# A written-out instruction order, numbered buffers and a finer softmax chain in a fused attention and highway kernel

## The chip, the cores and the metric

The kernel runs on one core of one Trainium2 chip. The core has five engines with instruction streams of their own: TensorE (PE in the profile, with its weight loads as PEld), VectorE (DVE), ScalarE (ACT), GpSimd (POOL) and SyncE (SP). Sixteen DMA engines move data between HBM and the core's memories; here GpSimd issues all loads and SyncE all stores. The metric is the device time in microseconds. The profile of one execution shows a span, from the first to the last instruction, which is a little shorter than the time.

## The reference

Four batches of N = 6336 rows with C = 256 channels. Channel attention: q and k are normalized over the rows, their 256 x 256 product is put through a softmax, and v is multiplied by it. The result x, 25344 rows of 256, goes through a highway layer.

```python
qn = q / (np.linalg.norm(q, axis=1, keepdims=True) + 1e-06)
kn = k / (np.linalg.norm(k, axis=1, keepdims=True) + 1e-06)
s = kn.transpose(0, 2, 1) @ qn / tau                 # [B, 256, 256]
a = np.exp(s - s.max(-1, keepdims=True))
a /= a.sum(-1, keepdims=True) + 1e-09
x = (v @ a).reshape(B * N, C)
H = np.maximum(x @ w_h, 0.0)
T = 1.0 / (1.0 + np.exp(-(x @ w_t + b_t)))
out = T * H + (1.0 - T) * x                          # float32
```

All inputs and the output are float32 in HBM, 25.95 MB for each of q, k, v and the output.

## The kernel before

Each batch has two stages. Stage 1 runs over 50 steps of 128 (at the end 96) rows and accumulates k'q, and the diagonals of k'k and q'q, in two PSUM banks. In batches 1 to 3, for the first five of the six chunks of eight steps, the sum of q squares is not made on TensorE: ScalarE squares and GpSimd adds. Then a chain of small operations makes the norms, the softmax and three 256 x 256 weight matrices in one tile pair `mr`: for x itself (times -0.5), for x w_h and for x w_t. Stage 2 runs over 25 tasks of 256 rows per batch, 100 tasks g in all: v is transposed, and three products h, t and d (x) are made, four matmuls of 256 columns each; ScalarE computes a halved relu into d's bank and a tanh, VectorE combines. Loads cast float32 to float16 on the way.

Everything is a task with engine, estimated duration, dependencies and buffers. A simulation at build time (`Plan.run`) picks, for each engine, the ready task with the lowest priority number, and the instructions are emitted in that order. At run time every engine runs its own instructions in order.

```python
QK_BUFS = 5; V_BUFS = 5; O_BUFS = 7; LAG = 5; UNTIL = 73; APART = 5
BY_DMA = 3          # last batch: chunks 3 to 6 of v are transposed by DMA
PRIO = {"tr": (24.974, 16.445, 34.195, 63.304), ...}      # offsets by kind and batch

def new(tag, shape, dt, name):
    return pool_of.get(tag, work).tile(shape, dt, tag=tag, bufs=nbuf[tag], name=name)

# [cut] first loads: q, k of batch 0, then
for s in range(0, CH, CH // 2):
    plan_load("q", 1, 0, s, CH // 2)
    plan_load("k", 1, 0, s, CH // 2)
w_ld = [...]                       # the two weight matrices
plan_load("v", 0, 0)

def stage1(b, s):                  # one step
    for c in range(2):
        nc.tensor.matmul(sg[c][:, 0:C], kc, qa, start=first, stop=False)
        nc.tensor.matmul(sg[c][:, C : C + P], kc, kc, start=False, stop=False)
        if not apart(b, s // CH):
            nc.tensor.matmul(sg[c][:, C + P : C + 2 * P], qa[:, cs], qa[:, cs], start=False, stop=last)

def sum_squares(b, j, step):       # GpSimd, per chunk of eight steps
    if step == 0:   add(out=sq, in0=sq, in1=other)                              # 1024 columns
    elif step == 1: add(out=sq[:, 0:2, :], in0=sq[:, 0:2, :], in1=sq[:, 2:4, :])  # 512
    else:                                                                       # 256, twice
        add(out=sq[:, 0, :], in0=sq[:, 0, :], in1=sq[:, 1, :])
        add(out=sums[b], in0=sums[b], in1=sq[:, 0, :])

# the chain of a batch
dq = dve(lambda: (diagonal(0), diagonal(1), rest_of_q()), ...)
nq = pool(lambda: norm(0), ...)                 # power 0.5 on GpSimd
dk = dve(lambda: (diagonal(2), diagonal(3)), ...)
nk = pool(lambda: norm(2), ...)
plan.loads_stop.append((stop, nk))              # no load is issued until nk is done
gs = act(copy_g, ...)                           # both halves, after dk
iq = dve(lambda: (recip(0), dcat()), ...)       # dcat: 2 x identity times inverse norm
ik = dve(lambda: recip(2), ...)
def recip(n):
    inv = st["inv"][:, n : n + 2]
    nc.vector.tensor_scalar(out=inv, in0=inv, scalar1=1e-6, scalar2=None, op0=AluOp.add, ...)
    nc.vector.reciprocal(out=inv, in_=inv)
def bcast():
    nc.tensor.matmul(st["cqb"], ones, st["dcat"][:, :, :], start=True, stop=True)
# [cut] scale, exp, transpose, recip_sum
def soft(c):                                    # x weights, VectorE
    nc.vector.tensor_scalar(out=mr_t[b][c][:, 0:C], in0=st["e"][:, c, :],
        scalar1=st["ri"][:, c : c + 1], scalar2=-0.5, op0=AluOp.mult, op1=AluOp.mult)
def evac_ah(c, e):                              # h and t weights, 512 columns at once
    o, a, r = mr_t[b][c][:, C : 3 * C], st["ah", c], st["ri"][:, c : c + 1]
    if e == "ACT": nc.scalar.mul(out=o, in_=a, mul=r)
    else:          nc.vector.tensor_scalar(out=o, in0=a, scalar1=r, ...)

# stores: chunk n is held back until chunk n + LAG has been begun (while that is at most UNTIL)
def hold(b, j):
    nc.sync.dma_start(out=held_row, in_=og[(b, j)][0:1, 0, :])

for x in plan.run():
    if x.fn is not None:
        x.fn()
```

Of the kernel before, what the change touches and what calls it, by code (L numbers as in the profile page):

```python
# [15 lines left out]
P = 128  # L16
# [6 lines left out]
AHEAD = 16  # L23
BY_DMA = 3
SHORT = 1.08
MOVE = 165e3
APART = 5
V_AHEAD = 2


PRIO = {
    "tr": (24.974, 16.445, 34.195, 63.304),
    "ev": (74.59, 73.008, 67.512, 50.704),
    "h": (-53.39, -86.015, -64.208, -14.641),
    "bias": (-28.394, 23.065, -1.772, 4.453),
    "t": (4.111, -1.918, 67.766, 74.312),
    "relu": (46.555, -20.175, -1.498, 14.915),
    "x": (0.958, -19.433, 43.343, -6.4),
    "gate": (-54.132, 37.28, -94.231, -112.222),
    "prod": (-40.861, -10.819, -26.763, -55.482),  # L40
    "res": (53.604, 18.42, 116.457, -9.113),
    "s1": (117.419, 42.459, 84.45),
    "sq": (-15.195, 72.384, 19.395),
}
POW = 0.75
HEAD = 5.5
TAIL = 66
EV = BIAS = ("ACT", "DVE")
ENDS = [18, 48.5, 62.25]


class Ring:


    def __init__(self, bufs):
        self.bufs = bufs
        self.freed = []

    def open_at(self, t):
        n = len(self.freed) - self.bufs  # L60
        return n < 0 or (self.freed[n] is not None and self.freed[n] <= t)


class Task:
# [3 lines left out]

    def __init__(self, eng, key, pitch, lat, deps, fn, take=(), drop=(), size=0, follows=()):
        self.eng, self.key, self.pitch, self.lat = eng, key, pitch, lat
        self.deps, self.fn, self.take, self.drop, self.size = deps, fn, take, drop, size
        self.follows = follows
        self.start = self.done = None
        self.late = 0.0
        self.soft = 0
        self.held = {}
        self.serial = False

    def engines(self):
        return self.eng if isinstance(self.eng, tuple) else (self.eng,)

    def settle(self, e):
        n = self.eng.index(e)
        self.pitch, self.lat = self.pitch[n], self.lat[n]
        self.fn = partial(self.fn, e)
        self.eng = e


class Plan:

# [8 lines left out]
    def __init__(self):  # L101
        self.tasks = []
        self.rings = {}

        self.loads_stop, self.sums_stop = [], []

    def ring(self, tag, bufs):
        self.rings[tag] = Ring(bufs)

    def add(self, *args, **kw):  # L110
        t = Task(*args, **kw)
        self.tasks.append(t)
        return t

    def run(self):
        queues = {"POOL": [], "SP": []}
        in_order = {"POOL": [], "SP": []}
        users, followers = {}, {}
        for n, x in enumerate(self.tasks):
            x.n, x.left, x.at = n, len(x.deps) + len(x.follows), 0.0  # L120
            for d in x.deps:
                users.setdefault(d, []).append(x)
            for d in x.follows:
                followers.setdefault(d, []).append(x)
            if x.size or x.serial:
                in_order[x.eng].append(x)
        for lst in in_order.values():
            lst.sort(key=lambda x: (x.key, x.n), reverse=True)
        engines = list(dict.fromkeys(x.eng for x in self.tasks if not isinstance(x.eng, tuple)))
        avail = {e: [x for x in self.tasks if e in x.engines() and not x.left and not (x.size or x.serial)] for e in engines}  # L130
        free = dict.fromkeys(engines, 2.1)
        lanes, order, events = [], [], [0.0, 2.1]
        t, left = 0.0, len(self.tasks)
        eps = 1e-6

        def ready(x):
            return (
                not x.left
                and x.at <= t + eps
                and all(self.rings[g].open_at(t + eps) for g in x.take)  # L140
                and (x.eng != "POOL" or not x.size or sum(d > t + eps for d in lanes) < self.LANES)
            )

        def finish(x, when):
            x.done = when
            events.append(when)
            for owner, tag in x.drop:
                self.rings[tag].freed[owner.held[tag]] = when
            release(users.get(x, ()), when)

        def release(us, when):
            for u in us:
                u.left -= 1
                u.at = max(u.at, when)
                if not u.left and not (u.size or u.serial):
                    for e in u.engines():
                        avail[e].append(u)

        def pick(e):
            quiet = held(self.sums_stop)  # L160
            best = min(
                (x for x in avail[e] if ready(x) and not (quiet and x.soft >= quiet)),
                key=lambda x: (x.key, x.n), default=None,
            )
            lst = in_order.get(e)
            if best is None and lst and ready(lst[-1]) and not (e == "POOL" and held(self.loads_stop)):
                return lst[-1]
            return best

        def held(stops):  # L170
            return next(
                (
                    n + 1 for n, (a, b) in enumerate(stops)
                    if a.start is not None and (b.done is None or b.done > t + eps)
                ),
                0,
            )

        while left or any(queues.values()):
            for e in engines:  # L180
                x = pick(e) if free[e] <= t + eps else None
                if x is None:
                    continue
                if x.size or x.serial:
                    in_order[e].pop()
                else:
                    for other in x.engines():
                        avail[other].remove(x)
                    if isinstance(x.eng, tuple):
                        x.settle(e)  # L190
                left -= 1
                x.start = t
                order.append(x)
                for g in x.take:
                    x.held[g] = len(self.rings[g].freed)
                    self.rings[g].freed.append(None)
                free[e] = t + x.pitch
                release(followers.get(x, ()), free[e])
                events.append(max(free[e], t + 2 * eps))
                if x.size:  # L200
                    queues[e].append([x, float(x.size), t + self.HEAD])
                    events.append(t + self.HEAD)
                    if e == "POOL":
                        x.lane = len(lanes)
                        lanes.append(1e9)
                else:
                    finish(x, t + x.lat)

            act = [qq for qq in queues.values() if qq and qq[0][2] <= t + eps]
            share = self.RATE / max(1, len(act))  # L210
            nxt = [x for x in events if x > t + eps] + [t + qq[0][1] / share for qq in act]
            assert nxt, "no task can start"
            nxt = min(nxt)
            for qq in act:
                qq[0][1] -= share * (nxt - t)
            t = nxt
            events = [x for x in events if x > t - eps]
            for qq in act:
                if qq[0][1] < 1.0:
                    x = qq.pop(0)[0]  # L220
                    finish(x, t + self.LAG + x.late)
                    if x.eng == "POOL":
                        lanes[x.lane] = t + self.LAG
        self.end = max(x.done for x in order)
        return order
# [3 lines left out]
def kernel(  # L229
# [37 lines left out]
        "sq": 2, "vT": 3, "vT_t": 1, "o": O_BUFS, "ot": 1, "uu": 3, "pp": 3, "vtsb": 9, "mr0": 2, "mr1": 2,  # L267
        "sg0": 1, "sg1": 1, "vt": 1, "t": 1, "h": 2, "d": 2,
# [6 lines left out]

    def new(tag, shape, dt, name):
        return pool_of.get(tag, work).tile(shape, dt, tag=tag, bufs=nbuf[tag], name=name)
# [64 lines left out]
    def plan_load(nm, b, j, s=0, n=CH):  # L342

        size = P * n * C * 4 if j < NJ else TR * 2 * C * 4
        tag = nm if j < NJ else f"tail_{nm}"
        x = plan.add(
            "POOL", len(plan.tasks), 0.54, 0, [], lambda: load(nm, b, j, s, n),
            take=[tag] if s == 0 else [], size=size * (1 if j < NJ and n > 2 else SHORT),
        )
        ld.setdefault((nm, b, j), []).append(x)  # L350
# [71 lines left out]
    def natural(b):  # L422

        return b == B - 1
# [670 lines left out]
```

## Time and profile before

Median 270.56 us of three runs (270.31 to 271.51); the span of the profile is 268.3 us.

| Part | Value |
|---|---|
| PE busy | 246.4 us (92%), 2430 matmuls |
| PEld busy | 216.6 us (81%) |
| VectorE busy | 181.6 us (68%) |
| ScalarE busy | 195.1 us (73%) |
| GpSimd busy | 131.7 us (49%) |
| granted TensorE clock, mean | 0.997 |
| first store issued | 101.0 us |
| last load issued | 221.3 us |
| last store issued | 264.6 us |

The page gives the busy share of each engine over 40 equal slices, one digit each in tenths; the DMA queues with the share of sixteen engines' time that their packets took; and a chain of waits, followed back from the last instruction. The windows cut the span into stretches. A busy TensorE there includes the overlap of pipelined matmuls, so a full row does not mean peak rate; the count of instructions beside it tells more.

### The profile page before, as it was taken

What the parts mean: (1) busy time and instruction counts of PE and PEld (TensorE: products, weight loads), DVE (VectorE), ACT (ScalarE), POOL (GpSimd) and SP (SyncE); (2) the same over time, 40 slices, a digit from 0 to 9 for tenths busy, and PEclk for the clock granted to TensorE, in tenths of its full rate; (3) what the DMA queues carried; (4) which work ended last, traced back from release to release, by engine and by line L of the source; (5) the groups of instructions that cost most, each with busy time, mean ns of one, the idle gap of its engine ahead of it and who ended that gap; (6) DMA issues with size and microseconds to landing.
All of it is one profiled execution on the core that took longest, in us unless ns stands there. A gap on an engine that the chain in (4) does not pass through costs nothing.

```text
span 268.3 us, 6249 instructions
## 1 busy us (share of the span) xinstructions
PE 246.4 (92%) x2430; PEld 216.6 (81%) x2430; DVE 181.6 (68%) x377; ACT 195.1 (73%) x365; POOL 131.7 (49%) x167
## 2 busy tenths in 40 slices
PE   0697977999999999999999999999999999999991
PEld 0596864889989978999999878999998778888880
DVE  1000035777766789557878797586878998998994
ACT  1001016978888789999898887787798999998980
POOL 7233468688778064695689138567655110000000
PEclk9999999999999999999999999999999999999998
DMA  6999999999999999999999999999999999999995
GB/s 107 215 211 208 206 206 202 212 213 214 214 213 212 213 214 255 247 263 269 275 286 258 267 267 254 249 236 281 287 280 239 284 214 304 379 399 165 351 423 232
DMA packets 24622, 67.24 MB, mean 251 GB/s; under 512 B 9104, under 2 KB 11280, under 8 KB 21648
## 3 DMA queue, kind: packets, MB, share of 16 engines
q0 software_dynamic: 13472, 39.20, 75.0%
q1 hardware_dynamic: 11120, 27.64, 29.0%
q8 instruction: 19, 0.31, 0.4%
q14 instruction: 11, 0.09, 0.1%
HBM read 78.38 MB, written 25.95 MB: 389 GB/s over the span
## 4 chain that ended last, share of the span: by engine, by line
PE 76%; DMA 12%; ACT 5%; POOL 2%; issue 2%; DVE 2%; ACTq 0%; DVEq 0%; POOLq 0%
PE h L800 16%; PE t L800 16%; PE d L800 15%; PE sg L452 12%; DMA k<-in_k_dram 10%; PE sg L453 6%; PE vtps L760 5%; DMA v<-in_v_dram 2%; ACT uu L854 2%; PE sg L455 2%; PE t L831 1%; PE vtps L754 1%; PE ah L689 1%; POOL q L327 1%; ACT d L840 1%
## 5 line engine op out<-in xcount | busy, mean ns | idle before, releaser
L800 PEld LDWEIGHTS <-vtsb 128*128 128x128 f16 (+1 forms) x1044 | 98.8, 99 | 17.3 <-issue 3.2
L452 PE MATMUL sg<-q,k 128*128 128x256 f16 x384 | 83.8, 277 | 12.7 <-DMA k<-in_k_dram 12.6
L861 DVE SCALAR_TENSOR_TENSOR pp<-uu,d 128x512 f32<-128x512 f32 (+1 forms) x100 | 68.0, 684 | 28.4 <-PE d L800 16.1
L453 PE MATMUL sg<-k 128*128 128x128 f16 x384 | 76.8, 223 | 0.0
L854 ACT ACTIVATE uu<-t 128x512 f32<-128x512 f32 (+1 forms) x100 | 59.7, 597 | 19.1 <-PE t L800 18.5
L880 DVE SCALAR_TENSOR_TENSOR o<-h,pp 128x512 f32<-128x512 f32 x96 | 65.5, 686 | 1.7
L840 ACT ACTIVATE d<-h 128x512 f32<-128x512 f32 (+1 forms) x100 | 57.9, 584 | 5.7 <-PE h L800 4.9
L800 PE MATMUL t<-mr,vtsb 128*128 128x256 f16 (+1 forms) x348 | 52.2, 272 | 1.5 <-ACT t L533 1.2
L800 PE MATMUL h<-mr,vtsb 128*128 128x256 f16 (+1 forms) x348 | 51.2, 272 | 0.5 <-ACT vtsb L533 0.5
L800 PE MATMUL d<-mr,vtsb 128*128 128x256 f16 (+1 forms) x348 | 51.5, 272 | 0.1
L452 PEld LDWEIGHTS <-k 128*128 128x128 f16 x384 | 38.0, 99 | 16.7 <-DMA k<-in_k_dram 13.9
L476 POOL TENSOR_TENSOR sq<-sq,sq 128x1024 f32<-128x1024 f32 x15 | 35.4, 2361 | 16.7 <-ACT sq L470 16.6
L453 PEld LDWEIGHTS <-k 128*128 128x128 f16 x384 | 38.0, 99 | 1.5
L533 ACT COPY t<-bias_all 128x512 f32<-128x512 f32 (+1 forms) x60 | 35.4, 591 | 1.4
L455 PE MATMUL sg<-q 128*128 128x128 f16 x144 | 32.5, 226 | 0.0
L470 ACT ACTIVATE sq<-q 128x1024 f32<-128x1024 f16 x30 | 31.3, 1053 | 0.0
L760 PE MATMUL vtps<-ident,v 128*128 128x128 f32 x144 | 27.8, 275 | 0.9 <-DMA v<-in_v_dram 0.6
L569 DVE SCALAR_TENSOR_TENSOR junk<-sg,ident 128x128 f32<-128x128 f32 x16 | 4.6, 288 | 33.2 <-PE sg L455 32.7
L535 DVE COPY vtsb<-vtps 128x256 f32<-128x256 f32 (+2 forms) x47 | 19.6, 418 | 7.0 <-PE vtps L760 6.7
L327 POOL DMA_DIRECT2D v<-in_v_dram x24 | 13.7, 571 | 18.9 <-PE vtps L760 11.7
L327 POOL DMA_DIRECT2D q<-in_q_dram x28 | 15.4, 552 | 15.1 <-DMA q<-in_q_dram 7.1
L327 POOL DMA_DIRECT2D k<-in_k_dram x28 | 15.3, 548 | 13.1 <-DMA k<-in_k_dram 9.2
(78 smaller groups left out, 249.5 us busy)
## 6 DMA issues: line engine op xcount, KB each, us to landing
out_dram<-o SPq DMA_DIRECT2D x23, 1024.0 KB, 9.6
v<-in_v_dram POOLq DMA_DIRECT2D x24, 512.0 KB, 16.6
q<-in_q_dram POOLq DMA_DIRECT2D x21, 512.0 KB, 16.2
k<-in_k_dram POOLq DMA_DIRECT2D x21, 512.0 KB, 18.0
q<-in_q_dram POOLq DMA_DIRECT2D x5, 256.0 KB, 9.6
k<-in_k_dram POOLq DMA_DIRECT2D x5, 256.0 KB, 8.9
out_dram<-o SPq DMA_DIRECT2D x2, 512.0 KB, 4.2
out_dram<-ot SPq DMA_DIRECT2D x4, 192.0 KB, 5.1
```

The source lines that it names most:

```text
L327: nc.gpsimd.dma_start(out=t[:, s : s + n, :], in_=main_rows(src)[:, j * CH + s : j * CH + s + n, :])
L452: nc.tensor.matmul(sg[c][:, 0:C], kc, qa, start=first, stop=False)
L453: nc.tensor.matmul(sg[c][:, C : C + P], kc, kc, start=False, stop=False)
L455: nc.tensor.matmul(sg[c][:, C + P : C + 2 * P], qa[:, cs], qa[:, cs], start=False, stop=last)
L476: add(out=sq, in0=sq, in1=other)
L533: nc.scalar.copy(out=out, in_=in_)
L760: nc.tensor.transpose(ps[:, u, 0:nr], v.bitcast(f32), ident0[0:nr, 0:nr])
L800: nc.tensor.matmul(out[0:nr, u, :], vt[u][kt][:, 0:nr], mr[kt][:, col * C : (col + 1) * C], **flags(u, kt))
L840: nc.scalar.activation(out=d[0:nr, :, :], in_=ps_t["h", b, i][0:nr, :, :], func=Act.Relu, scale=0.5)
L854: nc.scalar.activation(out=uu[0:nr, :, :], in_=ps_t.pop(("t", b, i))[0:nr, :, :], func=Act.Tanh, scale=-0.5)
L861: nc.vector.scalar_tensor_tensor(out=pp[0:nr, :, :], in0=el.pop(("uu", b, i))[0:nr, :, :], scalar=1.0, in1=ps_t.pop(("d", b, i))[0:nr, :, ...
L880: nc.vector.scalar_tensor_tensor(out=ot, in0=ps_t.pop(("h", b, i))[0:nr, :, :], scalar=0.0, in1=el.pop(("pp", b, i))[0:nr, :, :], op0=AluO ...
```

## The change

The order of instructions no longer comes from the simulation; it is a list of task names in the source, with the engine where there was a choice. Some further parts change with it:

- every buffer of a ring has a tag of its own, and buffers are given out in turn;
- the q squares are added into one running 1024-column accumulator and folded once per batch, instead of being folded per chunk;
- the small addition of 1e-6 to the norms is done column by column;
- the broadcast of inverse norms uses them directly as matmul weights against the identity; the diagonal tiles `dcat` are gone;
- the x weights are scaled by ScalarE with a factor that VectorE prepares;
- the chain is cut into finer tasks: single diagonals, copies of one half, h and t weights evacuated separately, each product waiting only for its own weights;
- the orders of loads, stores, holds and DMA transposes are part of the list. The same four chunks are transposed by DMA, and the same 17 tasks have their bias added on TensorE.

The code also gains forms (`FORM_B`, `FORM_D`, squares of k) that are switched off: their lists are empty.

```diff
-PRIO = { ... }
+BY_DMA = (3, 4, 5, 6)
+OFF = {"q": (0, 5, 5, 5), "k": (0, 0, 0, 0)}
+ON_PE = tuple(g for g in range(67, 100) if g % 2)
+FORM_B = ()
+FORM_D = ()
+ORDER = """
+Lk0.0 Lk0.1 Lq0.0 Lk0.6 const Lq0.1 Lk0.2 Lq0.2 Lb1 Lq0.6 Lb0 Lq0.3 s0.0 Lk0.3 s0.1 s0.2 s0.3 Lq0.4.0 s0.4
+[cut]
+s0.27 s0.28 s0.29 Lq0.5.6 s0.30 s0.31 Lk1.0.0 s0.32 s0.33 s0.34 Lq1.0.0 s0.35 s0.36 s0.37 Lw1 s0.38 spd1 s0.39
+Lw0 s0.40 s0.41 Lv0.0 s0.42 Lq1.0.4 s0.43 s0.44 s0.45 s0.46 s0.47 spd0 c0.dq0 c0.g0/ACT b0/ACT c0.dq1 c0.dk0
+c0.nq c0.dk1 sqq1.0.0 s1.0 c0.nk c0.iq c0.b c0.g1/ACT Lk1.0.4 c0.ik s1.1 Lv0.1 s1.2 c0.s0 s1.3 Lq1.1 c0.s1
+c0.e0 Lk1.1 c0.e1 c0.tr0 c0.r0 Lv0.2 c0.v0/ACT c0.tr1 c0.r1 Lq1.2 c0.f0 c0.v1/ACT c0.a0 Lk1.2 tr0 c0.h0/DVE
+c0.f1 ev0/ACT c0.t0/ACT tr2 c0.t1/DVE c0.a1 t0 ev2/ACT c0.h1/ACT tr1 g0 h0 ev1/DVE b1/DVE tr3 r0 h1 ev3/ACT t1
+[cut: some 1350 tasks]
+O3.4.0 p95 h97 g96 x96 y95 r97 t97 p96 b98/ACT x97 g97 h98 y96 t98 p97 r98 O3.5.0 h99 g98 x98 y97 r99 t99 p98
+x99 g99 y98 p99 O3.5.4 y99 O3.6
+"""
```

In the names, L is a load, s a step of stage 1, sq, ad and fs the squares, their additions and folds, c0 the chain of batch 0; tr and ev transpose v and evacuate it; b, h, t, x, r, g, p, y are bias, the three products, relu, gate and the two VectorE steps of a task; H, O and T are holds, stores and DMA transposes.

```diff
     def run(self):
-        [cut: the simulation]
+        for token in ORDER.split():
+            name, _, e = token.partition("/")
+            x = self.tasks[name]
+            x.fn(e) if e else x.fn()
 
     def new(tag, shape, dt, name):
-        return pool_of.get(tag, work).tile(shape, dt, tag=tag, bufs=nbuf[tag], name=name)
+        at = opened.get(tag, 0) % nbuf[tag]
+        opened[tag] = opened.get(tag, 0) + 1
+        return pool_of.get(tag, work).tile(shape, dt, tag=f"{tag}.{at}", bufs=1, name=name)
 
+    def add_square(nm, b, j, n, e):                 # acc is 1024 columns wide
+        eng.tensor_tensor(out=acc, in0=acc, in1=sq_t.pop((nm, b, j, n)), op=AluOp.add)
 
         def recip(n):
-            nc.vector.tensor_scalar(out=inv, in0=inv, scalar1=1e-6, ...)
+            for c in range(n, n + 2):
+                one = st["inv"][:, c : c + 1]
+                nc.vector.tensor_scalar(out=one, in0=one, scalar1=1e-6, ...)
             nc.vector.reciprocal(out=inv, in_=inv)
 
         def bcast():
-            nc.tensor.matmul(st["cqb"], ones, st["dcat"][:, :, :], start=True, stop=True)
+            for c in range(2):
+                nc.tensor.matmul(
+                    st["cqb"][:, c, :], st["inv"][:, c : c + 1].to_broadcast([P, P]), ident0,
+                    start=True, stop=True,
+                )
 
         def soft(c):
-            nc.vector.tensor_scalar(out=mr_t[b][c][:, 0:C], in0=st["e"][:, c, :],
-                scalar1=st["ri"][:, c : c + 1], scalar2=-0.5, op0=AluOp.mult, op1=AluOp.mult)
+            nc.scalar.mul(out=rows_of(c)[:, 0:C], in_=st["e"][:, c, :], mul=st["rm"][:, c : c + 1])
 
-        def evac_ah(c, e):
-            o, a, r = mr_t[b][c][:, C : 3 * C], st["ah", c], st["ri"][:, c : c + 1]
+        def evac_ah(c, n, e):
+            o = rows_of(c)[:, (n + 1) * C : (n + 2) * C]
+            a, r = st["ah", c][:, n * C : (n + 1) * C], st["ri"][:, c : c + 1]
 
     def hold(b, j):
-        nc.sync.dma_start(out=held_row, in_=og[(b, j)][0:1, 0, :])
+        at = 8 * (b * NJ + j)
+        nc.sync.dma_start(out=held_row[:, at : at + 8], in_=og[(b, j)][0:1, 0, 0:8])
```

## The prediction

> **What bounds the kernel now.** I read the page from the top: the 40 slices first, then the DMA queues and the chain of waits, and after that the same span cut into windows. The slices show two rows that are full from the first tenth on, PE and DMA; no slice has both slack in DMA and work waiting.
>
> ```profile
> PE   0697977999999999999999999999999999999991
> ...
> DMA  6999999999999999999999999999999999999995
> ...
> q0 software_dynamic: 13472, 39.20, 75.0%
> q1 hardware_dynamic: 11120, 27.64, 29.0%
> ...
> HBM read 78.38 MB, written 25.95 MB: 389 GB/s over the span
> ...
> PE 76%; DMA 12%; ACT 5%; POOL 2%; issue 2%; DVE 2%; ACTq 0%; DVEq 0%; POOLq 0%
> ```
>
> The loads' queue takes 75.0% and the stores' 29.0% of sixteen engines: together above 100%, so DMA has no idle stretch to speak of. The last line says that the chain that ended last ran on TensorE for 76% and waited for DMA for 12%. That 12% is in the head: the list of waits has TensorE waiting 12.6 us for k and the chain then 5.76 us for the first v. The windows say how full each resource is:
>
> ```profile
> 36.00:41.00 5.00, 3.04 (x32) 2.38 (x31) 3.02 (x16) 1.15 (x4) 3.48 (x6) 1.00 1.23 203
> 41.00:46.00 5.00, 3.75 (x30) 2.41 (x29) 3.12 (x9) 3.29 (x8) 3.85 (x6) 1.00 1.05 199
> 46.00:88.00 42.00, 41.74 (x415) 37.16 (x413) 29.42 (x51) 36.57 (x65) 33.13 (x38) 1.00 1.07 213
> ...
> 235.00:240.00 5.00, 4.99 (x49) 4.17 (x48) 4.72 (x8) 4.43 (x9) 0.00 (x0) 1.00 1.02 428
> 240.00:245.00 5.00, 5.00 (x48) 4.30 (x46) 4.45 (x9) 4.66 (x9) 0.00 (x0) 1.00 1.19 200
> ...
> 255.00:260.00 5.00, 5.00 (x47) 4.37 (x46) 4.66 (x8) 4.52 (x10) 0.00 (x0) 1.00 1.00 419
> ```
>
> Columns: busy PE, PEld, DVE, ACT, POOL, then clock, DMA share and GB/s on the core's side. Until 100 us only loads run; each writes half of what it reads (float32 becomes float16), so 213 GB/s is 426 GB/s of reading. At 255 us, 5 us before TensorE ends, stores still run at 419 GB/s. So two budgets end almost together.
>
> **The TensorE budget.** Rows of the chain give a group of four products as 0.44 us; spaced in the timeline they stand 0.437 apart. 300 groups x 0.437 = 131; stage 1: 80 full steps x 0.44 = 35, 120 without the q square x 0.34 = 41; 87 transpose pairs x 0.22 = 19; 17 bias products x 0.22 = 4; four chains at about 2, and sums, 9. Sum about 239 us. The first matmul starts near 9 us and the last ends at 262.6: 253.6 us, so about 14 us are lost. In the head (9 to 45.65, where the first h starts) the work done is 22 + 8 x 0.34 + 2 = 27 of 36.6, so 10 are lost there; the rest of the kernel loses only 4 to 5, mostly around the three later chains, where the windows lack busy time (148 to 160: 11.07 of 12).
>
> **The DMA budget.** 78.38 + 25.95 = 104.3 MB at the 422 GB/s of the load-only stretch (to 100 us, 20.4 MB written, 40.8 read, in 96.7 us) take 247 us. DMA runs from about 2.5 to 266 us: 263.5. The missing 16 are: some 10 us for the four DMA transposes (the 200 GB/s window at full share, and its neighbour), some loss where loads and stores mix, and 2 to 3 us of true slack: 220 to 225 at share 0.95, and the end, where the last stores wait for VectorE.
>
> **What the Trainium skill says.** "Perfetto Trace Analysis", section "Identifying the Most-Contended Engine", says that matmul occupancy is a poor measure, because matmuls are pipelined, and that DMA is to be judged by HBM utilization. The trace agrees: the row calls TensorE 10.00 busy of 10 us in windows with 91 and with 109 matmuls. "DMA: Bandwidth & Descriptors", section "Issuing engines are not separate DMA queues", says that DMAs from all engines run on the same sixteen and interleave; the sum of 104% agrees, so moving stores between or behind loads makes no bandwidth. The same page, section "Bandwidth", gives 425 GB/s for 16 MB; the 422 here lie there, so there is little above it to win. "GPSIMD Engine Reference", section "Elementwise — side-by-side cycle accounting", has a two-input add of 2048 columns at 4497 ns; the 1024-column add here took 2361 ns, which agrees, and the change trades exactly these.
>
> **The change part by part.**
>
> *Order of the first loads.* Before, the first v is issued at 38.88 us, behind both halves of q and k of batch 1 and the weights, and, GpSimd being in order, behind both power operations of the first norm (37.52 to 39.0). It lands about 44.64. Afterwards its load stands ahead of the chain and of the second halves: 2 x 128 x 1024 x 4 B = 1.05 MB less ahead of it, 1.05/0.42 = 2.5 us. It should land at about 42.1.
>
> *The chain of batch 0.* It starts at 36.7 (last stage-1 matmul) and its last evacuation ends at 44.9 (VectorE 43.42 + 1.51 for both halves). Removed: two multiplications that build the diagonal (0.48 us together); the broadcast now takes the inverse norms as weights against the identity. Added: one small addition (0.16) with each reciprocal, so net -0.3. The scaling of the x weights goes from VectorE (2 x 0.347) to ScalarE, with one more 0.15 us multiplication on VectorE; it lies beside the transposes, so 0 on the path. The evacuations of 512 columns (0.75 us each, in series on VectorE = 1.51) become four of 256 (0.37 to 0.42 by the rows of equal size), split over two engines: 0.8 in parallel, so -0.7. The first v transposes and gates no longer wait for all of it: t needs only its own two quarters. And the square of 2.0 us that ScalarE runs at 42.28 in the middle of the chain now stands before it. With e ended near 41.2 instead of 41.65, I get the last quarter at about 43.4 instead of 44.9. First products therefore at about 43.2 instead of 45.65: -2.4 us of TensorE time.
>
> *The three later chains.* The same shortening is off the path there, as stage 2 of the batch before fills TensorE. What it saves is part of the 4 to 5 us of small losses; I give it 1 us.
>
> *Squares.* Before, per chunk: one 2361, one 1283, two of 730 ns: 74.4 us in all. After: 27 adds x 2361 = 63.7, and six folds, 6.0: 69.7. GpSimd was 49% busy, so -4.7 us there is worth nothing by itself; ScalarE keeps its 30 squares (31.3 us).
>
> *Buffers numbered one by one.* They are given out in the same turn as before and in the same number; no transfer gets a buffer earlier by it. I count 0.
>
> *Stores, holds and transposes.* The count of bytes is the same: four chunks of the last batch are still transposed by DMA. Stores of batches 0 to 2 come in bursts, and the transposes are asked for near task 77, 79, 86 and 87 instead of roughly 79 to 94. DMA then always has something queued around 220 us and at 250; it can win back about 1.5 of the 2 to 3 us of slack.
>
> Sum on TensorE: -2.4 - 1.0 = -3.4 us. On DMA: not more than about -3. The later of the two counts, so I take -3.0 to -3.3 from 270.56: 267.3 us.
>
> **The rivals.**
>
> *DMA swallows it.* TensorE starts stage 2 earlier by 2.4 us but the stores still end when the DMA engines have moved 104 MB and four transposes. For it: 419 GB/s at 255 to 260 us, shares of 1.0 and more all along. Against it: the dip at 220 us, and 299 to 364 GB/s in the last microseconds of stores. It would give 269 to 270.
>
> *The frozen order waits.* Engines run strictly in written order; where a real duration differs from the one for which the order was written, an engine stands behind an instruction that isn't ready. Most exposed are VectorE and ScalarE in the last batch, 9.4 and 9.1 of 10 busy, and GpSimd, where a load stands behind a 2.36 us add that waits for a square. For it: ScalarE gets 8 scalings more just where it is full (212 to 220: 7.67 of 8). Against it: the kernel before is in-order too, its order was merely computed at build time, and a load takes 16 us from issue to landing, so a delay of 3 us is covered. It would give 271 to 273.
>
> *Both budgets give more.* If the losses after 46 us (4 to 5 us) vanish whole and the transposes disturb stores less, 264 to 265 is reached; below lies the DMA floor: 2.5 + 247 + 10 + 2 = 261.5 of span, plus the 2.3 between span and time, 263.8.
>
> **Range and chances.** Predicted 267.3, between the main sum and a partial swallowing by DMA. The range of 8 in 10 goes from 264.3 (nearly the floor) to 270.3 (all swallowed). A gain over 2% means under 265.1, only 1.3 us above the floor: 0.17. Slower by over 2% means over 276, which would need waits of 5 us that no part of the old trace shows: 0.04. Within 2%: 0.79.
>
> **What would show it.** Right: the first v lands near 42 us and the first h or t product starts near 43; the group of 512-column evacuations is gone and sixteen of 256 take about 0.4 each; the DMA row stays full and HBM traffic rises to about 393 GB/s; TensorE's last product is near 259. Wrong: if the first product comes at 43 and TensorE ends at 259 but the last store lands as late as before, DMA swallowed it; if ScalarE or VectorE show new waits, or the load queue's share sinks below full in the middle, the written order is at fault; if the time falls below 264, my DMA floor is wrong, by the mixed or the transposing stretches.

## The result, and the profile after

| | before | changed |
|---|---|---|
| time, median of four runs each, same chip | 270.96 us | 268.55 us |
| ratio, 95% interval | | 0.9913 (0.989 to 0.9935) |
| span of the profile | 268.3 | 267.1 |
| first product of stage 2 | 45.65 | 44.02 |
| TensorE's last product ends | 262.6 | 259.4 |
| last store issued | 264.6 | 261.15 |
| last store issued to end of span | 3.7 | 5.95 |

Faster by 0.9%. TensorE ends 3.3 us earlier and the last store is issued 3.45 us earlier, but the span is only 1.2 us shorter and the time 2.4 us. These lines of the changed kernel's page (slices, queues, chain of waits) answer to those shown of the kernel before:

```profile
PE   0298988999999999999999999999999999999980
...
DMA  6999999999999999999999999999999999999995
...
q0 software_dynamic: 13472, 39.20, 74.7%
q1 hardware_dynamic: 10912, 27.63, 29.3%
...
HBM read 78.38 MB, written 25.95 MB: 391 GB/s over the span
...
PE 77%; DMA 13%; DVE 4%; POOL 2%; issue 1%; ACT 1%; DVEq 0%; POOLq 0%
```

The last slice of the PE row has gone to 0: TensorE is done while the DMA row is still busy. The windows of the changed kernel (busy PE, PEld, DVE, ACT, POOL, clock, DMA share, GB/s) show where:

```profile
36.00:41.00 5.00, 3.63 (x37) 2.84 (x35) 2.89 (x18) 3.03 (x7) 3.34 (x6) 1.00 1.18 207
41.00:46.00 5.00, 4.39 (x25) 2.39 (x25) 2.53 (x9) 4.07 (x12) 1.78 (x4) 1.00 1.10 215
...
148.00:160.00 12.00, 12.00 (x121) 10.80 (x119) 9.35 (x32) 10.61 (x24) 7.45 (x10) 1.00 1.05 263
...
230.00:235.00 5.00, 5.00 (x53) 4.45 (x51) 4.74 (x9) 4.98 (x10) 0.53 (x1) 1.00 0.96 188
...
245.00:250.00 5.00, 5.00 (x46) 4.28 (x45) 4.67 (x8) 4.52 (x9) 0.00 (x0) 1.00 0.84 241
250.00:255.00 5.00, 5.00 (x48) 4.38 (x46) 4.66 (x8) 4.53 (x10) 0.00 (x0) 1.00 1.01 418
255.00:260.00 5.00, 4.38 (x39) 3.67 (x36) 4.80 (x8) 3.96 (x8) 0.00 (x0) 1.00 1.00 410
260.00:265.00 5.00, 0.00 (x0) 0.00 (x0) 1.09 (x2) 0.00 (x0) 0.00 (x0) 0.83 0.86 329
```

The same windows of the kernel before:

```profile
148.00:160.00 12.00, 11.07 (x112) 9.78 (x111) 9.55 (x32) 9.97 (x23) 3.01 (x5) 1.00 1.06 270
...
260.00:265.00 5.00, 2.34 (x19) 1.80 (x17) 4.37 (x7) 1.60 (x4) 0.00 (x0) 1.00 0.89 364
```

Around the third chain (148 to 160) TensorE is busy throughout, where it had lost 0.9 of 12 us; in the long stretches beside it (100 to 148, 160 to 200) it now loses 0.3 and 0.4 us, where it had lost nothing. From 250 us the stores run at 410 to 418 GB/s until after TensorE has ended, and in 260 to 265 at 329 with no matmul left.

**Where TensorE won its 3.3 us.** A busy row can't say it. I used the lag: the time of an event less the TensorE work that stands before it in the order. The work is counted with fixed durations, nearly those of the prediction (0.437 us per product group, 0.44 or 0.33 per step of stage 1, and so on, 238.3 us in all). With the same durations for both kernels, a smaller growth of the lag means that TensorE lost less time.

| event | lag before | lag changed | grown since the last row |
|---|---|---|---|
| first product of stage 2 | 18.2 | 17.7 | |
| broadcast, chain of batch 1 (99.4; 99.8 us) | 20.6 | 18.8 | 2.4; 1.1 |
| broadcast, chain of batch 2 (156.8; 155.5) | 22.2 | 19.5 | 1.6; 0.7 |
| broadcast, chain of batch 3 (211.0; 208.7) | 22.9 | 20.6 | 0.7; 1.1 |
| last product (262.6; 259.4) | 24.4 | 21.1 | 1.5; 0.5 |

The head gave 0.5, although the first product comes 1.6 us earlier: before, TensorE had done eight steps of batch 1's stage 1 while it waited, now only four. The other 2.8 us came after 46 us.

Half of these 2.8 us stand in the lists of TensorE's waits (what waited, for what; us in total, times, longest). The kernel before, 46 to 263 us:

```profile
PE t L800 <- ACT t L533: 1.2, 3, 0.7
PE vtps L760 <- ACT vtsb L533: 0.3, 1, 0.3
PE d L800 <- ACT d L840: 0.3, 1, 0.3
PE t L800 <- ACT d L840: 0.2, 1, 0.2
```

The changed kernel, 46 to 260 us:

```profile
PE h L728 <- ACT mr L634: 0.6, 2, 0.3
```

All are waits for ScalarE. The first line is its copy of the bias into t, and 0.9 of those 1.2 us lie at the third chain. So 1.4 us of the gain are 2.0 us of waits less 0.6; the list does not show where the rest was lost.

### The profile page after: what moved, and what is told of

Same layout as the page of the kernel before. It is cut to its first block, busy times and chain, and to the rows that moved or that the text cites. A ratio compares the mean times of both kernels' runs of the same rounds, so it can differ in the third digit from the quotient of the medians.

```text
span 267.1 us, 6250 instructions
## 1 busy us (share of the span) xinstructions
PE 243.9 (91%) x2438; PEld 216.4 (81%) x2438; DVE 183.4 (69%) x380; ACT 198.7 (74%) x378; POOL 127.4 (48%) x143
## 4 chain that ended last, share of the span: by engine, by line
PE 77%; DMA 13%; DVE 4%; POOL 2%; issue 1%; ACT 1%; DVEq 0%; POOLq 0%
PE h L728 15%; PE t L728 15%; PE d L728 15%; PE sg L372 13%; DMA k<-in_k_dram 9%; PE sg L374 7%; PE vtps L688 6%; DMA q<-in_q_dram 3%; PE sg L376 2%; DVE pp L815 2%; PE t L768 1%; DVE o L861 1%; PE vtps L682 1%; POOL k L261 1%; PE eps L610 1%
## 5 line engine op out<-in xcount | busy, mean ns | idle before, releaser
L403 POOL TENSOR_TENSOR acc_q<-acc_q,sq_q 128x1024 f32<-128x1024 f32 x27 | 64.0, 2371 | 36.2 <-ACT sq_q L397 35.7
L785 ACT ACTIVATE d<-h 128x512 f32<-128x512 f32 (+1 forms) x100 | 58.5, 587 | 9.4 <-PE h L728 7.5
L728 PE MATMUL d<-mr,vtsb 128*128 128x256 f16 (+1 forms) x348 | 52.1, 272 | 0.0
L481 ACT COPY t<-bias_all 128x512 f32<-128x512 f32 (+1 forms) x57 | 33.7, 592 | 1.1
L376 PE MATMUL sg<-q 128*128 128x128 f16 x144 | 31.9, 221 | 0.0
L397 ACT ACTIVATE sq_q<-q 128x1024 f32<-128x1024 f16 x27 | 28.5, 1056 | 0.0
L483 DVE COPY t<-bias_all 128x512 f32<-128x512 f32 (+1 forms) x26 | 18.0, 692 | 6.4 <-ACT uu L804 5.8
L483 DVE COPY vtsb<-vtps 128x256 f32<-128x256 f32 (+2 forms) x45 | 18.8, 418 | 4.8 <-PE vtps L688 4.6
```

The lines of the kernel that those rows point to most:

```text
L403: eng.tensor_tensor(out=acc, in0=acc, in1=sq_t.pop((nm, b, j, n)), op=AluOp.add)
L481: nc.scalar.copy(out=out, in_=in_)
L483: nc.vector.tensor_copy(out=out, in_=in_)
L728: nc.tensor.matmul(out[0:nr, u, :], vt[u][kt][:, 0:nr], mr[kt][:, col * C : (col + 1) * C], **flags(u, kt))
L785: nc.scalar.activation(out=d[0:nr, :, :], in_=h[0:nr, :, :], func=Act.Relu, scale=scale)
```

## The experiments

All ratios are against the kernel before, in runs on the same chip in alternation; the trials ran on two chips, so ratios compare better than times. The changed kernel's own ratio is 0.9913. Three questions: what sets the end, what the early v and the chain's parts do, and whether something beats both.

### What sets the end: two stores left out

Both kernels without the stores of batch 2's chunks 4 and 5, so that 2.1 MB of the output isn't written.

```diff
     def store(b, j, s, n):
+        if (b, j) in ((2, 4), (2, 5)):
+            return
```

> The changed kernel without the stores of two chunks (2.1 MB, batch 2, chunks 4 and 5), so a part of the output isn't written. If the DMA engines' remaining work sets the end, 2.1 MB at 0.42 MB per us are 5 us of work, of which the end can shorten until the last store's own way is left: the last store is issued at 261.2 and needs at least 2.7, so about 264 of span, 3 us less: 265.5. If TensorE and VectorE set the end, the time stays at 268.5 within 0.5.

> The kernel before without the stores of the same two chunks (2.1 MB, batch 2, chunks 4 and 5; a part of the output isn't written). Its last store is issued at 264.6 and the span ends 3.7 us later, where the changed kernel needed 5.9 us. If only what is left for the DMA engines counts, both kernels fall alike, by 2 to 3 us. If the kernel before is held by TensorE and the changed one by DMA, this one falls by about 1 us (3.7 less the 2.7 that the last store needs), ratio about 0.996.

Changed kernel: 266.35 us, ratio 0.9847 (0.9816 to 0.9878), by the ratios 1.8 us less than with them and by the spans 2.6. Kernel before: 270.66 us, ratio 1.0012 (1.0002 to 1.0022), nothing gained. The DMA queue's own timeline has the last stores of the changed kernel

```profile
247.07 13.10 SPq L875 DMA_DIRECT2D out_dram<-o  x7
261.15 0.33 SPq L873 DMA_DIRECT2D out_dram<-ot  x1
```

and without the two stores

```profile
240.95 19.32 SPq L877 DMA_DIRECT2D out_dram<-o  x7
261.24 0.33 SPq L875 DMA_DIRECT2D out_dram<-ot  x1
```

and of the kernel before, without these two (with them: 264.60)

```profile
264.90 0.33 SPq L894 DMA_DIRECT2D out_dram<-ot  x1
```

(start, duration of the merged issues). In the changed kernel the last issue stands where it did, and so does TensorE's last product (259.5), yet the span ends at 264.5 instead of 267.1. So it was the queue of bytes that ended late. From the last issue to the end 3.3 us remain here, 3.7 and 3.8 in the kernel before with and without its two stores: that is a lone last store's own way. The changed kernel's 5.95 hold about 2.4 us of backlog. The kernel before was held by TensorE and the last VectorE steps; the changed one is held by DMA.

### Filling the hole in the DMA row

```diff
-... r86 T3.5 t86 ... T3.6 ... O3.0.0 ... O3.1.0 ...
+... r86 O3.0.0 O3.1.0 T3.5 t86 ... T3.6 ...
```

> The changed kernel with the first two stores of the last batch issued ahead of its third DMA transpose instead of behind its fourth. In the changed kernel DMA is at a share of 0.84 from 245 to 250 us and then runs full until the end, 5.9 us after the last store was issued. If the DMA engines' remaining work sets the end, filling that hole brings 0.8 us and up to 1.5: 267 to 267.7, ratio near 0.987. If TensorE and VectorE set the end, nothing changes: 268.5. If the transposes suffer from the stores beside them, products of the last chunks wait for transposed v and the time rises.

269.07 us, ratio 0.995 (0.9918 to 0.9982): no gain; the medians are 0.5 us worse, but the intervals of the two ratios overlap. The third expectation came true. The list of TensorE's waits from 245 to 256 us has one entry:

```profile
PE h L728 <- DMA vT<-v: 2.1, 1, 2.1
```

The transpose issued behind the two stores landed late; TensorE ended 2.4 us later, at 261.7, and the backlog had shrunk by about as much: from the last issue (263.5) 3.9 us remain, and the span is 267.4. In this stretch a store ahead of a transpose is paid for by TensorE, one behind it by the end.

### The early v

Undone in the changed kernel:

```diff
-Lw0 ... Lv0.0 s0.42 Lq1.0.4 ... c0.nq ... c0.nk ... Lk1.0.4 c0.ik s1.1 Lv0.1
+Lw0 ... s0.42 Lq1.0.4 Lk1.0.4 ... c0.nq ... c0.nk ... c0.ik s1.1 Lv0.0 Lv0.1
```

> The changed kernel with the first load of v back where it was: behind both second halves of q and k of batch 1 and behind both power operations of the first norm. If the early v gives the gain of the head, v lands about 2.5 us later, the first product of stage 2 starts near 45.5 us instead of 44.0 and TensorE ends 1.5 us later, near 261; the time then rises by 1 to 1.5 us, ratio about 0.996. If the chain sets the start and v was hidden, the first product stays within 0.7 us of 44.0. If the end is set by what the DMA engines still have to move, the time stays within 0.5 us of the changed kernel (268.5) even where TensorE ends later.

271.46 us, ratio 1.0034 (0.9991 to 1.0076): the whole gain is gone. TensorE's timeline in the chain of batch 0:

```profile
45.24 0.66 PE L688 MATMUL vtps<-ident,v 128*128 128x128 f32 x2 [2.54 <-DMA v<-in_v_dram]
45.70 1.06 PE L622 MATMUL ah<-wht,et 128*128 128x512 f16 x2
46.55 0.63 PE L688 MATMUL vtps<-ident,v 128*128 128x128 f32 x2
46.98 0.42 PE L728 MATMUL t<-mr,vtsb 128*128 128x256 f16 x1
```

The bracket is idle time and what ended it. In the written order the first v transpose stands between the chain's two last matmul groups (ah), so a late v holds the chain too. The first product comes at 46.98, and from there to the last product (262.4) the lag is 3.0 us larger than in the changed kernel.

Then the opposite: only the early v, in the kernel before. The first trial moved v ahead of the weights as well:

```diff
+    order.remove(v0)
+    order.insert(order.index(q1), v0)       # q1: second half of q, batch 1
+    # the four steps that need the halves: behind the second fold
```

> The kernel before, its own order, with two moves only: the first load of v ahead of the second halves of q and k of batch 1 and of the norms, and the four steps of stage 1 that need those halves put behind the last of the chain's matmuls. If an early v is by itself worth what I counted for the head (2.4 us of TensorE time), the first product comes near 43.5 us instead of 45.65, TensorE ends about 2 us earlier and the time falls by 1 to 2 us, ratio about 0.994. If the old chain, which ends at 44.9, sets the start, the first product comes at 45.2 at best, and the time stays within 0.5 us of the kernel before.

273.45 us, ratio 1.0112 (1.0088 to 1.0137). This tells nothing of v: TensorE waited 2.0 us for `wht`, which my move had pushed back. Mended:

```diff
+    order[n:n] = [v0, q4]                   # n: behind both weights
+    order.insert(order.index(norms[1]) + 1, k4)
+    # the four steps: behind the first x product
```

> Replaces the earlier trial with an early v, in which the two weight matrices had slipped behind v. The kernel before, its own order, with the first v right behind the weights and ahead of the second halves of q and k of batch 1 and of the norms, and the four steps of stage 1 that need those halves behind the first complete task of stage 2. If an early v is by itself worth the 2.4 us that I counted for the head, the first product comes near 43.5 instead of 45.65, TensorE ends 2 us earlier and the ratio is about 0.993. If the old chain sets the start (44.9) and the four steps had only filled the wait, the first product comes at 44.5 to 45.2, 1.4 us of steps have to be made up later, and TensorE ends where it did or up to 0.7 us later: ratio 1.000 to 1.003.

269.99 us, ratio 1.0002 (0.9979 to 1.0026). The first product came at 44.61, 1.0 us earlier, and TensorE ended at 262.8 as before: what was won was the four steps that now had to be made up. An early v is worth nothing to the old order and is indispensable to the new one.

### The parts of the chain

All at once in the changed kernel, with the diagonal tiles built where the broadcast stands:

```diff
         def bcast():
+            for c in range(2):
+                nc.vector.tensor_scalar(out=st["dcat"][:, c, :], in0=ident0, scalar1=inv_c, ...)
-                nc.tensor.matmul(st["cqb"][:, c, :], inv_c.to_broadcast([P, P]), ident0, ...)
+            nc.tensor.matmul(cqb, ones, st["dcat"][:, :, :], ...)
         def soft(c):
-            nc.scalar.mul(...)
+            nc.vector.tensor_scalar(...)
         def evac_ah(c, n, e):               # once for 512 columns
```

> The changed kernel, same written order, with the old form of the chain: diagonal tiles built by VectorE, x weights scaled by VectorE, h and t weights evacuated together in one operation of 512 columns. If the finer chain is what removed TensorE's losses around the chains (between 45 and 156 us the lag of TensorE behind its own work grew by 4.0 us before and by 1.8 after), the lag grows again by 1.5 to 2.5 us, TensorE ends near 261.5 and the time rises by 1.5 to 2 us, ratio near 0.998. If the new order alone removed them, the lag stays and the time is within 0.5 us of 268.5.

277.52 us as the median of runs that spread from 273.5 to 278.9; the ratio, 1.0168 (1.0105 to 1.0232), is of the faster ones alone, and the profiled run is of the slower kind, so only the waits around the chains are read in it. Then one part at a time.

Evacuation of 512 columns alone:

> The changed kernel with one part of the finer chain undone: h and t weights evacuated together, 512 columns in one operation on the engine that had the first of the two. If these evacuations are what cost the time when the whole chain was made coarse (277.5), this alone brings 2 to 5 us. If it was the place of the diagonal tiles in VectorE's order, this brings at most 1 us: 268.5 to 269.5.

268.64 us, ratio 0.9935 (0.9921 to 0.9949), TensorE's end at 259.65.

Diagonal tiles alone, straight behind the inverse norms:

> The changed kernel with the diagonal tiles back, built by VectorE straight behind the inverse norms of q, as in the kernel before, and broadcast through the ones matrix. When the whole chain was made coarse, the tiles had been built later, where the broadcast stands, and the time was 277.5. If it was that place in VectorE's order, this variant costs at most the 0.5 us of the two operations per chain and is within 0.5 us of the changed kernel (268.5). If the diagonal tiles themselves were the cost, it is at 272 or above.

268.37 us, ratio 0.9932 (0.9905 to 0.9959), TensorE's end at 259.3.

Scaling of the x weights on VectorE alone:

> The changed kernel with the x weights scaled by VectorE again, at the same place of the written order. If moving them to ScalarE took them off the path, the time rises by 0.5 to 1 us. By my count they lie beside the transposes: within 0.3 us of 268.5. If VectorE's in-order stream carries them past a gap that the order had left for other work, TensorE waits for them around each chain and the time rises by 2 us or more; that would be the larger part of what the coarse chain cost.

268.87 us, ratio 0.9944 (0.9926 to 0.9962), TensorE's end at 259.4. None of the three costs anything that shows. What the coarse chain cost lies then, by exclusion, in where the diagonal tiles were built; the tiles at that place alone were not run, so a joint effect of the parts isn't ruled out. The coarse chain's list of TensorE's waits from 46 to 230 us has one entry:

```profile
PE cqb L562 <- DVE dcat L558: 4.8, 3, 3.4
```

In this run TensorE ended at 266.0, 6.6 us later than in the changed kernel, and these waits are 4.8 of them. From the last issue (267.8) to the end of the span another 9.4 us pass, which isn't explained here. VectorE's and GpSimd's rows around its third chain, from the timeline:

```profile
156.07 3.79 DVE L558 TENSOR_SCALAR dcat<-ident,inv 128x128 f32<-128x128 f32 x2
...
157.37 2.40 POOL L403 TENSOR_TENSOR acc_q<-acc_q,sq_q 128x1024 f32<-128x1024 f32 x1
```

and TensorE's row for the broadcast:

```profile
160.01 0.67 PE L562 MATMUL cqb<-dcat,ones 128*128 128x256 f32 x2 [3.37 <-DVE dcat L558]
```

Two operations that take 0.28 us each elsewhere took 3.79 together and ended at 159.86, just behind GpSimd's addition (159.77); TensorE stood 3.37 us for them. At the chain before, one took 0.61 and ended at 100.75, again within 0.1 us of the end of a GpSimd addition (100.66). The Trainium skill, "SBUF — State Buffer", section "Who interferes with whom", says that VectorE in its two-port modes and GpSimd share a pair of ports as an exclusive lock, that `tensor_scalar` can enter such a mode, and that the loser blocks for the other's whole instruction. The ends agree with that, also those of the x weights' scalings on VectorE: two of them, 0.34 us elsewhere, took 0.60 and 0.84 under an addition and ended within 0.2 us of its end. Their pace fits a double-rate mode: from 128 to 256 columns these operations, which read and write SBUF, grow from 0.28 to 0.345 us, about 0.5 ns per column, while the weights' evacuations from PSUM grow from 0.48 us at 256 columns to 0.75 at 512, about 1.05 ns per column (estimates from these durations; the output types differ). That these forms held the ports isn't shown by itself, and the additions don't explain the start of the longest operation: it began at 156.26, 1.1 us before the addition, while GpSimd was issuing loads. What held it until then stays open. In the kernel before (at 155.3 us, with no addition on GpSimd) the same operations took 0.28 each. The change takes them out of VectorE altogether.

### A version that beats both

The end is DMA's, and TensorE has about 2 us to spare (the backlog). So chunk 3 of the last batch goes from DMA transposes back to TensorE. First trial, tasks inserted by a fixed rule, evacuations on VectorE and ScalarE in turn:

```diff
-BY_DMA = (3, 4, 5, 6)
+BY_DMA = (4, 5, 6)
-T3.3
+tr87 ... ev87/DVE, tr88 ... ev88/ACT, tr89 ... ev89/DVE, tr90 ... ev90/ACT
```

> The changed kernel with chunk 3 of the last batch transposed by TensorE (four tasks of 0.22 us, four evacuations on VectorE and ScalarE in turn) instead of by DMA. The four DMA transposes cost about 10 us of DMA time for 26 steps, so a chunk of 8 steps 3 us. If what is left for the DMA engines sets the end, the end comes 1.5 to 2.2 us earlier although TensorE ends 0.9 us later: 266.3 to 267. If TensorE, ScalarE and VectorE in the last batch set it, the time rises by 0.9 us or more, to 269.4.

269.32 us, ratio 0.9966 (0.9952 to 0.9979). TensorE ended at 262.7: the transposes stood too close to the evacuations of those before them.

```profile
PE vtps L682 <- ACT vtsb L481: 1.2, 1, 1.2
PE vtps L682 <- DVE vtsb L483: 0.5, 1, 0.5
```

Second trial, one task of distance, all on VectorE:

```diff
+... t84 p83 tr87 h85 g84 ev87/DVE x84 ... b86/ACT tr88 h86 g85 ev88/DVE x85 ...
+... p85 tr89 h87 g86 ev89/DVE x86 ... b88/ACT tr90 x87 g87 ev90/DVE h88 ...
```

> Chunk 3 of the last batch transposed by TensorE as in the earlier trial, but with each transpose one task after the evacuation of the one before and all four evacuations on VectorE. In that trial TensorE stood 1.7 us and more for evacuations between 237 and 245 us and ended at 262.7. If those waits were the cost, TensorE now ends near 260.3, the last store is issued near 262 and needs 3.3 to 3.8: a span of 265.4 to 265.9, a time near 267 and a ratio near 0.987. If VectorE has no room for the four evacuations (4.67 of 5 busy there), TensorE ends at 261.5 or later and the time is at 268.5 or above.

267.23 us (267.05 to 267.41), ratio 0.9884 (0.9858 to 0.991). The lowest run of the two variants on the same chip that come to the time of the changed kernel (268.37 and 268.87) was 268.14, so it beats these by 0.4 and 0.6% and the kernel before by 1.2%. Against the changed kernel itself, which was not run beside it, the ratios give 0.3% with intervals that overlap, and the spans 267.1 and 265.4. TensorE ends at 260.4, and its windows show the DMA queue below full at the end:

```profile
255.00:260.00 5.00, 5.00 (x46) 4.43 (x44) 4.69 (x8) 4.15 (x8) 0.00 (x0) 1.00 0.82 331
260.00:265.00 5.00, 0.40 (x4) 0.15 (x2) 2.08 (x4) 0.59 (x1) 0.00 (x0) 0.95 0.43 159
```

Shares of 0.82 and 0.43 stand where the changed kernel had 1.00 and 0.86. The span ends 3.2 us after the last issue (262.17), so the backlog is gone.

## Why the prediction was right, and where it was not

- *The total.* 267.3 was predicted and 268.55 measured. The forecast of TensorE's end, near 259, was met (259.4), but by luck: it is the sum of two terms, -2.4 and -1.0, that measured -0.5 and -2.8.
- *The head, -2.4 us of TensorE time.* Measured 0.5 by the lag. I counted how much earlier the first product comes and not what TensorE had done while it waited: four steps of stage 1 fewer, 1.4 us, less 0.2 for a pair of transposes done earlier. The first product also came at 44.0, not 43.2. The term that failed there is the -0.7 for evacuations in quarters: they took 0.48 to 0.50 us each, not the 0.37 to 0.42 of a copy of that size, the last of them ended at 45.0 where the operations of 512 columns had ended at 44.9, and with those put back alone the first product came at 43.8. v was no longer waited for, as predicted.
- *The three later chains, -1 us.* Measured 2.8 between 46 us and the end. Evacuation, diagonal tiles and scaling, each put back alone, left TensorE's end where it was (259.3 to 259.65). So the gain isn't in any one of these parts; by exclusion it is in the order, in which the place of each operation fits what the other engines do. The waits for ScalarE, 2.0 us before and 0.6 after, agree with that. It is argued and not shown: I didn't run the old chain whole in a fitting order, nor the numbered buffers or the running accumulator of the q squares by themselves.
- *Stores, holds and transposes, up to 1.5 us of slack won back.* This failed. The holes moved, to 230 to 235 (share 0.96) and 245 to 250 (0.84), where the queue stands behind transposes, and a backlog of 2.4 us was left at the end.
- *The rival "DMA swallows it"* was right in kind and half in size. Of 3.3 us, the profile shows 1.2 left in the span and the runs 2.4 in the time. The ratio for two stores fewer (0.9847 against 0.9913, and 1.0012 in the kernel before) shows the change of the bound from TensorE to DMA. I had DMA's gain as "not more than about -3" and should have taken the later of the two ends, with the last store's own 3.2 to 3.8 us, instead of the sum on TensorE.
- *"The frozen order waits"* didn't happen in the changed kernel: TensorE waits 0.6 us in all for other engines between 46 and 260 us. The trials show it for small edits: a late v costs 3.0 us of lag, an evacuation one place too late 1.7 us of waits, a diagonal tile at a bad place 3.4.
- *Buffers 0, squares 0.* GpSimd's busy time fell from 131.7 to 127.4 us, about the 4.7 counted; none of TensorE's waits above is for it.

## What to carry to other kernels

When two resources end together, work out the end of each separately and take the later: here 3.3 us won on TensorE gave 2.4 in the time, and the next gain came from giving TensorE more work (0.9 us of transposes) to relieve DMA. Measure progress on a full engine by its lag behind the work in its own order; a start that comes earlier is no gain if the filler that stood before it has to be made up. In a hand-written order each placement leans on others (v early and fewer fillers; transposes one task behind evacuations), so a part of it undone alone shows what the order relies on and not what the part brings.

## What the runs showed of the hardware

- The same VectorE operation of 128 columns took 0.28 us, 0.61 and once about 3.6 (the longest of eight), the two long ones ending within 0.1 us of the end of a GpSimd addition.
- From the issue of a last store of 192 KB to the end of the span 3.1 to 3.9 us passed in eight kernels (the kernel before and its three variants; the changed kernel with two stores fewer, with two stores earlier and in both trials with chunk 3 on TensorE), and 4.25 in the one with the late v.
- In the changed kernel a scaled evacuation of 128 x 256 (h and t weights) took 0.46 to 0.54 us on ScalarE, where a copy of the same size took 0.35 to 0.41; on VectorE the two took 0.47 to 0.49 and 0.41 to 0.43.
